# Separate PSUM tiles for inverse results and totals, earlier loads of batch 1, and a respread last stage in a Fourier and routing kernel

## The chip, the cores and the metric

One core of one Trainium2 chip runs the whole program. The metric is device time in microseconds (us) of one execution, the median of several. TensorE is called PE here, VectorE DVE, ScalarE ACT, GpSimd POOL and SyncE SP, as the profile names them.

## The reference, cut to what matters

Eight batches of x (3136 by 256) go through a real FFT along the sequence, a complex linear layer with a soft threshold, and the inverse FFT. Then a gate scores every row, the 128 rows of highest score in each batch go through a two-layer network, and their result is added with a sigmoid gate.

```
X = rfft(x, axis=1)
Yr = soft(Xr @ w_r - Xi @ w_i + b_r, 0.01)
Yi = soft(Xr @ w_i + Xi @ w_r + b_i, 0.01)
y = irfft(Yr + 1j*Yi, n=3136, axis=1)
scores = y @ w_gate
top = the 128 rows of highest score of each batch
out = y;  out[top] += sigmoid(scores[top]) * (relu(y[top] @ w1) @ w2)
```

## The kernel before, in words

The length 3136 is split as 98 by 32. Each batch passes through these stages, as matmuls against small tables:

- `ld_x` loads a pair of column groups into one of two `xts` tiles (of batch 0, the second half into the two `cvs` tiles), three DMAs each; `fold` adds and subtracts the two halves (POOL, in batch 0 partly DVE); `s1` multiplies (8 matmuls into PSUM tile `s`), ACT copies the result to SBUF, and three DMAs store a pair of results to the scratch `As`. There are U = 8 units `i` per batch.
- `ld_a` reads `As` back in another order, and `s2` makes the spectrum of group `g` (G = 13 groups per batch, the last one narrow): 32 matmuls into `px`, ACT casts the high part `Xh` (L450), DVE subtracts for the low part `Xl` (L451).
- `spectral` multiplies with the weights in three products of six matmuls: `k1` first (into `pc`), which ACT copies to `ks` (L465) and POOL adds to the bias in `kb` (L467), then two into `py`, to which DVE adds `kb` (L471).
- `shrink` is the soft threshold: ACT makes `r` (L476), DVE makes `Y` (L478).
- `s2i` is the first inverse stage of a group: 16 matmuls (L496, the narrow group L500) into `pc`, an ACT copy of both halves to `ct` (L502), and for each half a DVE multiply-and-sum with the gate vector (L505) that leaves the scores of the group in `Csc`. `ct` is stored to the scratch `Cs`.
- `ld_c` reads `Cs` back, and `s1i` is the last inverse stage (8 matmuls into `s`, L544, and an ACT copy to `ot`, L546); pairs are stored to the output (L553, L554).
- `route` (one generator per batch) makes the scores (`score`), finds the threshold four bits at a time (`select`: nine rounds, each a matmul of totals, L244, read by DVE, L247 or L254, and two longer DVE counts, L237 and L241) and the row numbers (`place`, L267 to L314). Its matmuls write `sel_ps` and `route_ps`, which are columns of `pc`.
- `fetch` gathers the 128 rows (L322), and `ffn` runs the network on them (`prepare`, `hidden`, `combine`) and scatters them.

[...] `pc` is one tile of two banks with four users: the left half of its first bank and the left half of its second are the two halves of the result of `s2i`, the right half of the first is `sel_ps` and `route_ps`, and the right half of the second is `k1`. The waits between engines are made by the tile framework, from which instructions read and write a tile.

The order on every engine is the order in which the program is written (`manual_schedule`). After a prologue for batch 0, one loop runs over steps `t`. A step flushes the pending stores and issues the loads (all on SP's queue), and then runs: `s2` of group t+1; `pair` (one `s1` or `s1i`); `tick(threads)`, which moves every active route generator on by one yield; `spectral` of group t, with a second tick after `k1`; the folds; `tick(ffns)`; `s2i` of group t-1; `shrink` of group t; and `pair` again. So a route generator moves by two yields a step, and its totals matmul stands on PE's queue between `s2` and `k1`. Batch 1 runs its `s1` by the table `first` during the first steps, later batches LEAD = 17 steps ahead by `steady`, and `s1i` follows LAG = 18 steps behind, eight units in 13 steps.

Of the kernel before, what the change touches and what calls it, by code (L numbers as in the profile page):

```python
# [10 lines left out]
F32 = mybir.dt.float32  # L11
# [8 lines left out]
B, S, D = 8, 3136, 256  # L20
# [80 lines left out]
def fourier_moe(ctx: ExitStack, tc: tile.TileContext, x, w_r, w_i, b_r, b_i, wg, w1, w2,  # L101
# [11 lines left out]
    xv = x.rearrange("b (h m c) d -> b m h c d", h=2, c=N2)  # L113
    ov = [o.rearrange("(a r c i) d -> c a r (i d)", r=16, c=2, i=2) for o in outs]
    As, Cs, xt, sd, at, ct, av, cv, ot, X, Y, Csc = [{} for _ in range(12)]
    pc = ps.tile([128, 2, 512], F32, name="pc", bufs=1)

    def c_tile(shape, dt, name):
        return const.tile(shape, dt, name=name)
# [26 lines left out]
    def ld(out, src):  # L146
        nc.sync.dma_start(out=out, in_=src)

    sel_ps, route_ps = pc[:, 0, D:D + 64], pc[:, 0, D + 64:]

    w3 = []

# [220 lines left out]
    def ld_x(b, i):  # L373
        if i % 2:
            return
        k = i // 2
        t = xt[b, k] = (cvs if b == 0 and k > 1 else xts)[k % 2].rearrange("p (h c) d -> p h c d", h=2)
        for r in range(2):
            ld(t[64 * r:64 * r + 48], xv[b, :48, :, 8 * k + 4 * r:8 * k + 4 * r + 4, :])
        ld(t[48:113:64], xv[b, 48, :, 8 * k:8 * k + 8, :].rearrange("h (r c) d -> r h c d", r=2))  # L380

# [71 lines left out]
    def spectral(b, g, between):  # L453
        r = 128 if width(g) == 2 else NF
        xh, xl = X.pop((b, g))

        def product(out, c, w):
            for h in range(2):
                mm3(out, xh[:, h, c, :], xl[:, h, c, :], w[0][:, h, :], w[1][:, h, :], start=(h == 0), stop=(h == 1))

        k1 = pc[:, 1, D:]
        py = ps.tile([128, 2, D], F32, name="py", bufs=1)
        product(k1, 2, wts[0])
        ks = pool.tile([128, 1, D], F32, name="ks", bufs=2)
        nc.scalar.copy(out=ks[:r, 0, :], in_=k1[:r])  # L465
        kb = pool.tile([128, 2, D], F32, name="kb", bufs=KB)
        nc.gpsimd.tensor_tensor(out=kb[:r], in0=ks[:r].broadcast_to([r, 2, D]), in1=bias[:r], op=ALU.add)  # L467
        between()
        product(py[:, 0, :], 1, wts[2])
        product(py[:, 1, :], 0, wts[1])  # L470
        nc.vector.tensor_tensor(out=py[:r], in0=py[:r], in1=kb[:r], op=ALU.add)  # L471
        return py, r
# [8 lines left out]
    def s2i(b, g):  # L481
        w = width(g)
        if g == 0:
            Cs[b] = dram.tile([NH, 64, D], F32, name="Cs")
            Csc[b] = pool.tile([128, NJ], F32, name="Csc")
            nc.vector.memset(Csc[b][:, NJ - 1:], 0.0)
        if g % 2 == 0:
            ct[b] = pool.tile([128, 4, D], F32, name="ct", bufs=3)
        y = Y.pop((b, g))
        r = 128 if w == 2 else 64  # L490
        p = pc[:, :, :D]
        if w == 2:
            for c in range(2):
                for q in range(2):
                    for a in range(2):
                        nc.tensor.matmul(p[64 * a:64 * a + 64, q, :], gi_sb[64 * q:64 * q + 64, g, c, 64 * a:64 * a + 64], y[64 * q:64 * q + 64, c, :],  # L496
                                         start=(c == 0), stop=(c == 1))
        else:
            for c in range(2):
                nc.tensor.matmul(p[:64, 0, :], gti_sb[:, c, :], y[:64, c, :], start=(c == 0), stop=(c == 1))  # L500
        o = 2 * (g % 2)
        nc.scalar.copy(out=ct[b][:r, o:o + w, :], in_=p[:r, :w])  # L502
        for k in reversed(range(w)):
            junk = pool.tile([128, D], F32, name="junk", bufs=1)
            nc.vector.tensor_tensor_reduce(out=junk[:r], in0=p[:r, k, :], in1=wgb[:r], scale=1.0, scalar=0.0,  # L505
                                           op0=ALU.mult, op1=ALU.add, accum_out=Csc[b][:r, 2 * g + k:2 * g + k + 1])
        t = ct[b]
        if w == 1:
            stores.append(lambda: nc.sync.dma_start(out=Cs[b][48], in_=t[:r, o, :]))
        elif g % 2 == 1:  # L510
            stores.append(lambda: nc.sync.dma_start(out=Cs[b][:48].rearrange("(j q) n d -> (q n) j d", q=2)[:, 2 * g - 2:2 * g + 2], in_=t))
# [15 lines left out]
    def ld_c(b, i):  # L527
        if i % 2:
            return
        k = i // 2  # L530
        t = cv[b, k] = (xts if b == B - 1 and k > 1 else cvs)[k % 2]
        for r in range(2):
            ld(t[64 * r:64 * r + 48], Cs[b][:48, 16 * k + 8 * r:16 * k + 8 * r + 8, :])
        ld(t[48:113:64], Cs[b][48, 16 * k:16 * k + 16].rearrange("(r n) d -> r n d", r=2))

    def s1i(b, i):
        e = i % 2
        if e == 0:
            ot[b] = pool.tile([128, 2, 2, 2 * D], F32, name="ot", bufs=2)
        f = cv[b, i // 2]  # L540
        p = ps.tile([128, 2, 2 * D], F32, name="s", bufs=1)
        for r in range(2):
            for c in range(2):
                nc.tensor.matmul(p[64 * c:64 * c + 64, r, :], w[64 * r:64 * r + NH, 2, :], f[64 * r:64 * r + NH, 4 * e + 2 * c:4 * e + 2 * c + 2, :], start=True, stop=True)  # L544
        t = ot[b]
        nc.scalar.copy(out=t[:, :, e, :], in_=p)  # L546
        if e == 0:
            return

        def store():  # L550
            n = slice(2 * i - 2, 2 * i + 2)
            for c in range(2):
                nc.sync.dma_start(out=ov[b][c, :48, n, :], in_=t[64 * c:64 * c + 48].rearrange("p r s x -> p (r s) x"))  # L553
            nc.sync.dma_start(out=ov[b][:, 48, n, :], in_=t[48:113:64].rearrange("p r s x -> p (r s) x"))  # L554
        stores.append(store)

    def warm():
        pf = pool.tile([128, 512], F32, name="Y", bufs=YB)
        nc.vector.memset(pf, 0.5)
        pr = pool.tile([128, 768], F32R, name="Xh", bufs=XB)  # L560
        nc.scalar.copy(out=pr[:, :512], in_=pf)
        p = ps.tile([128, 2, 512], F32, name="px", bufs=1)
        for i in range(30):
            nc.tensor.matmul(p[:, i % 2], pr[:, :128], pr[:, :512], start=True, stop=True)

    HB, YB, XB, KB, RB = 2, 2, 2, 1, 1
# [6 lines left out]
    def route(b):  # L573
        while done["s2i"] < b:
            yield
            yield
        yield
        yield
        yield from score(b)
        yield from select(b, 4, thrs)  # L580
        yield from place(b, thrs[b], slots)
# [50 lines left out]
    for i in range(U):  # L632
        fold(0, i, nc.gpsimd if i % 3 == 2 else nc.vector)
        s1(0, i)
        flush()
    weights()
    warm()
    ld_a(0, 0)
    consts_g(1)
    first = {i * 10 // U: i for i in range(U)}  # L640
    ld_x(1, 0)
    ld_x(1, 2)
    fold(1, 0, nc.gpsimd)
    fold(1, 1, nc.gpsimd)
    for t in range(-1, B * G + LAG + 1):
        flush()
        for b, i in steady(t + LEAD + 4):
            ld_x(b, i)
        if t + 2 in first and first[t + 2] > 2:
            ld_x(1, first[t + 2])  # L650
        if 1 < t + 3 < B * G:
            ld_a(*divmod(t + 3, G))
        for b, i in due(t - LAG + 2, U):
            ld_c(b, i)
        if t % 2 == 0 and (t + 4) // 2 in range(2, 7):
            consts_g((t + 4) // 2)
        if t == -1:
            consts_gi(0)
        if t % 2 and (t + 1) // 2 in range(0, 6):
            consts_gi((t + 1) // 2 + 1)  # L660
        if t == 8:
            consts_b()
        if t % 2 == 0:
            consts_moe((t - 14) // 2)
            split_moe((t - 18) // 2)
        if 0 <= t + 1 < B * G:
            s2(*divmod(t + 1, G))
        pairs = [(s1, b, i) for b, i in steady(t + LEAD)]
        if t in first:
            pairs.append((s1, 1, first[t]))  # L670
        pairs += [(s1i, b, i) for b, i in due(t - LAG, U)]

        def pair():
            if pairs:
                f, b, i = pairs.pop(0)
                f(b, i)
                if f is s1i and i == U - 1:
                    done["s1i"] = b

        pair()  # L680
        tick(threads)
        if 0 <= t < B * G:
            py, r = spectral(*divmod(t, G), lambda: tick(threads))
        else:
            tick(threads)
        for b, i in steady(t + LEAD + 2):
            fold(b, i, nc.gpsimd)
        if t + 2 in first and t >= 0:
            fold(1, first[t + 2], nc.gpsimd)
        tick(ffns)  # L690
        if 0 <= t - 1 < B * G:
            s2i(*divmod(t - 1, G))
            if (t - 1) % G == G - 1:
                done["s2i"] = (t - 1) // G
        if 0 <= t < B * G:
            shrink(*divmod(t, G), py, r)
        pair()
# [31 lines left out]
```

## Time and profile before

| what | us |
|---|---|
| median of three runs (902.44 to 913.03) | 906.48 |
| the profiled execution's own time | 905.22 |
| its span, first to last instruction | 903.4 |
| PE busy in the span | 700.4 |
| DVE, ACT, POOL busy | 501.2, 365.2, 309.3 |

The profiled execution is 1.8 us longer than its span and 1.3 us under the median. Busy times are unions over an engine's instructions. In a timeline row, a bracket gives the idle time of that engine before the row and what ended it. In a row of groups, the number behind the second bar is the idle time of the engine just before that group, with what ended it. In a row by stretch stand its two ends, its length, the busy time and count of PE, of its weight loads, of DVE, ACT and POOL, then the granted clock of PE (1 is 2.4 GHz), the DMA share and the rate in GB/s. DMA share is the mean busy share of the 16 DMA engines, and it can exceed 1 where packets overlap on an engine.

### The profile page before, as it was taken

To read this page: it belongs to the slowest core of one execution; us is meant where nothing else is said; L and a number is where in the kernel's file an instruction comes from. 1 tells how busy PE (TensorE), PEld (TensorE's weight loads), DVE (VectorE), ACT (ScalarE), POOL (GpSimd) and SP (SyncE) were. 2 spreads that over 40 slices of the span, in tenths; PEclk is the share of its full clock that TensorE was granted. 3 is DMA by queue.
4 is the path that set the end of the run, shared out by engine and by line. 5 is a ranking of instruction groups with operands and counts; after the bars stand their busy time and mean duration, and the time that the engine had idled before them with its cause. 6 is when DMAs were issued, how large, how long until landed. Compare 5 with 4: busy or idle time off the path is not lost.

```text
span 903.4 us, 20480 instructions
## 1 busy us (share of the span) xinstructions
PE 700.4 (78%) x8302; PEld 516.7 (57%) x8302; DVE 501.2 (55%) x1369; ACT 365.2 (40%) x579; POOL 309.3 (34%) x272
## 2 busy tenths in 40 slices
PE   4788798887877887788878887878878787678574
PEld 1456576555655665556655665656656666565243
DVE  4334455666367645675467645675466644774631
ACT  2244454445345444444344444444444333333120
POOL 3063654355433423443334424443232211221000
PEclk9889799999899999999999999999999998999567
DMA  8889989989887978977797977978786635755840
GB/s 166 231 184 225 248 196 218 239 197 249 198 199 192 211 160 200 226 173 177 176 212 198 211 169 186 223 170 198 168 185 158 158 87 139 156 138 118 188 112 14
DMA packets 87868, 163.83 MB, mean 181 GB/s; under 512 B 7809, under 2 KB 61052, under 8 KB 81502
## 3 DMA queue, kind: packets, MB, share of 16 engines
q1 hardware_dynamic: 86734, 160.26, 75.5%
q0 software_dynamic: 896, 2.17, 0.8%
q8 instruction: 65, 1.06, 0.5%
q14 instruction: 29, 0.24, 0.1%
q10 hardware_dynamic: 144, 0.10, 0.0%
HBM read 84.45 MB, written 78.12 MB: 180 GB/s over the span
## 4 chain that ended last, share of the span: by engine, by line
PE 43%; DVE 19%; ACT 9%; DMA 5%; issue 5%; POOL 1%; SPq 1%; POOLq 0%; ACTq 0%
PE pc L496 8%; DVE Xl L451 6%; DVE junk L505 6%; PE pc L218 5%; PE py L218 5%; PE py L219 5%; PE py L220 5%; ACT ct L502 4%; DVE Y L478 4%; PE m L347 3%; PE s L544 3%; PE pc L220 2%; PE pc L219 2%; ACT ot L546 2%; DMA cv<-Cs 2%
## 5 line engine op out<-in xcount | busy, mean ns | idle before, releaser
L467 POOL TENSOR_TENSOR kb<-ks,bias 128x512 f32<-128x512 f32 (+1 forms) x104 | 133.1, 1280 | 447.7 <-ACT ks L465 447.7
L471 DVE TENSOR_TENSOR py<-py,kb 128x512 f32<-128x512 f32 (+1 forms) x104 | 72.7, 699 | 196.0 <-POOL kb L467 127.4
L387 POOL TENSOR_TENSOR sd<-xt 113x512 f32<-113x512 f32 x114 | 143.3, 1278 | 48.7 <-DMA xt<-in_x 48.7
L502 ACT COPY ct<-pc 128x512 f32<-128x512 f32 (+1 forms) x104 | 59.0, 567 | 228.0 <-PE pc L496 215.9
L218 PE MATMUL pc<-wsh,Xh 128*128 128x256 f32 x208 | 74.1, 356 | 90.2 <-DVE ok L254 59.2
L505 DVE CUSTOM_DVE_ANT_0 junk<-pc,wgb 128x256 f32<-128x256 f32 (+1 forms) x200 | 84.8, 424 | 87.7 <-ACT ct L502 83.3
L218 PEld LDWEIGHTS pc<-wsh,Xh 128*128 128x128 f32 x208 | 42.9, 206 | 124.4 <-DVE ok L254 61.7
L496 PE MATMUL pc<-Y,gi_sb 64*64 64x256 f32 x1536 | 106.1, 392 | 0.0
L451 DVE TENSOR_TENSOR Xl<-px,Xh 128x768 fp32r<-128x768 f32 x96 | 91.2, 950 | 26.8 <-ACT Xh L450 26.3
L465 ACT COPY ks<-pc 128x256 f32<-128x256 f32 (+1 forms) x104 | 38.7, 372 | 148.0 <-PE pc L220 146.8
L444 PEld LDWEIGHTS px<-g_sb,av 64*64 64x64 f32 x3072 | 78.9, 134 | 29.9 <-issue 13.5
L444 PE MATMUL px<-g_sb,av 64*64 64x96 f32 x3072 | 85.4, 245 | 9.8 <-DMA av<-As 7.2
L398 PE MATMUL s<-sd,w 49*64 49x512 f32 x480 | 74.6, 647 | 20.7 <-DVE sd L387 10.4
L450 ACT CAST Xh<-px 128x768 fp32r<-128x768 f32 x96 | 76.9, 801 | 12.3 <-PE px L444 12.3
L546 ACT COPY ot<-s 128x1024 f32<-128x1024 f32 x64 | 65.1, 1017 | 38.0 <-PE s L544 31.9
L544 PE MATMUL s<-cv,w 49*64 49x512 f32 x480 | 71.5, 631 | 10.7 <-ACT ot L546 8.2
L476 ACT ACTIVATE r<-py,m2l 128x512 f32<-128x512 f32 (+1 forms) x104 | 71.8, 691 | 13.0 <-DVE py L471 13.0
L478 DVE SCALAR_TENSOR_TENSOR Y<-py,r 128x512 f32<-128x512 f32 (+1 forms) x104 | 71.3, 686 | 1.9 <-ACT r L476 1.8
L400 ACT COPY at<-s 128x1024 f32<-128x1024 f32 x58 | 59.7, 1030 | 22.9 <-PE s L398 22.9
L496 PEld LDWEIGHTS pc<-Y,gi_sb 64*64 64x64 f32 x1536 | 49.9, 134 | 25.6 <-issue 2.4
L218 PE MATMUL py<-wnh,Xh 128*128 128x256 f32 x208 | 63.9, 307 | 0.0
L220 PE MATMUL py<-wnl,Xh 128*128 128x256 f32 x208 | 63.9, 307 | 0.0
(128 smaller groups left out, 1352.6 us busy)
## 6 DMA issues: line engine op xcount, KB each, us to landing
av<-As SPq DMA_DIRECT2D x96, 256.0 KB
Cs<-ct SPq DMA_DIRECT2D x48, 512.0 KB
out<-ot SPq DMA_DIRECT2D x64, 384.0 KB
xt<-in_x SPq DMA_DIRECT2D x60, 384.0 KB
As<-at SPq DMA_DIRECT2D x60, 384.0 KB
cv<-Cs SPq DMA_DIRECT2D x60, 384.0 KB
cv<-in_x SPq DMA_DIRECT2D x4, 384.0 KB
As<-ot SPq DMA_DIRECT2D x4, 384.0 KB
```

Source lines behind the costliest of these rows:

```text
L218: nc.tensor.matmul(out, wh, mh, start=start, stop=False)
L220: return nc.tensor.matmul(out, wh, ml, start=False, stop=stop).ins
L387: eng.tensor_tensor(out=f[:113, k], in0=t[:113, 0], in1=t[:113, 1], op=op)
L444: nc.tensor.matmul(o[:, :, N2 * j:N2 * j + N2], a[64 * p:64 * p + 64, 2 * (g % 2) + j, 128 * h + 64 * q:128 * h + 64 * q + 64], g_sb[64 * ...
L451: nc.vector.tensor_tensor(out=vl, in0=v, in1=vh.bitcast(F32), op=ALU.subtract)
L467: nc.gpsimd.tensor_tensor(out=kb[:r], in0=ks[:r].broadcast_to([r, 2, D]), in1=bias[:r], op=ALU.add)
L478: nc.vector.scalar_tensor_tensor(out=y[:r], in0=py[:r], scalar=0.0, in1=r1[:r], op0=ALU.min, op1=ALU.add)
L496: nc.tensor.matmul(p[64 * a:64 * a + 64, q, :], gi_sb[64 * q:64 * q + 64, g, c, 64 * a:64 * a + 64], y[64 * q:64 * q + 64, c, :], start=(c ...
L502: nc.scalar.copy(out=ct[b][:r, o:o + w, :], in_=p[:r, :w])
L505: nc.vector.tensor_tensor_reduce(out=junk[:r], in0=p[:r, k, :], in1=wgb[:r], scale=1.0, scalar=0.0, op0=ALU.mult, op1=ALU.add, accum_out=C ...
L544: nc.tensor.matmul(p[64 * c:64 * c + 64, r, :], w[64 * r:64 * r + NH, 2, :], f[64 * r:64 * r + NH, 4 * e + 2 * c:4 * e + 2 * c + 2, :], st ...
L546: nc.scalar.copy(out=t[:, :, e, :], in_=p)
```

## The change

Three parts. In PSUM, the tile `pc` becomes two tiles of one bank, `pca` (first half of the `s2i` result, `sel_ps`, `route_ps`) and `pcb` (second half, `k1`); the ACT copy of the `s2i` result becomes two, the second half first, each followed by its DVE sum. At the beginning, two `ld_x` of batch 1 are issued among the stores of batch 0, the table `first` starts one step later and runs one unit per step, the other loads of batch 1 are issued earlier against it, and the warm-up has 14 matmuls for 30. At the end, `route` yields twice less, `s1i` runs one unit per step once the last group is through, the loads of the last batch stand in two groups (the first pair into the `xts` tiles), its `s1i` results take two `at` and two `ot` tiles, and its odd units write `px` for `s`.

```diff
-    pc = ps.tile([128, 2, 512], F32, name="pc", bufs=1)
+    pca, pcb = [ps.tile([128, 2 * D], F32, name=n, bufs=1) for n in ("pca", "pcb")]
...
-    sel_ps, route_ps = pc[:, 0, D:D + 64], pc[:, 0, D + 64:]
+    sel_ps, route_ps = pca[:, D:D + 64], pca[:, D + 64:]
...
-        for r in range(2):
+        for r in (1, 0):
             ld(t[64 * r:64 * r + 48], xv[b, :48, :, 8 * k + 4 * r:8 * k + 4 * r + 4, :])
...
-        k1 = pc[:, 1, D:]
+        k1 = pcb[:, D:]
...
-        p = pc[:, :, :D]
+        p = [t[:, :D] for t in (pca, pcb)]
...
-        nc.scalar.copy(out=ct[b][:r, o:o + w, :], in_=p[:r, :w])
         for k in reversed(range(w)):
+            nc.scalar.copy(out=ct[b][:r, o + k, :], in_=p[k][:r])
             junk = pool.tile([128, D], F32, name="junk", bufs=1)
-            nc.vector.tensor_tensor_reduce(out=junk[:r], in0=p[:r, k, :], in1=wgb[:r], scale=1.0, scalar=0.0,
+            nc.vector.tensor_tensor_reduce(out=junk[:r], in0=p[k][:r], in1=wgb[:r], scale=1.0, scalar=0.0,
...
-        t = cv[b, k] = (xts if b == B - 1 and k > 1 else cvs)[k % 2]
+        t = cv[b, k] = (xts if b == B - 1 and k < 2 else cvs)[k % 2]
...
-            ot[b] = pool.tile([128, 2, 2, 2 * D], F32, name="ot", bufs=2)
+            ot[b] = pool.tile([128, 2, 2, 2 * D], F32, name="at" if b == B - 1 and i < 4 else "ot", bufs=2)
...
-        p = ps.tile([128, 2, 2 * D], F32, name="s", bufs=1)
+        p = ps.tile([128, 2, 2 * D], F32, name="px" if b == B - 1 and e else "s", bufs=1)
...
-        for i in range(30):
+        for i in range(14):
             nc.tensor.matmul(p[:, i % 2], pr[:, :128], pr[:, :512], start=True, stop=True)
...
         while done["s2i"] < b:
             yield
             yield
-        yield
-        yield
         yield from score(b)
...
         s1(0, i)
+        if i == 4:
+            ld_x(1, 0)
+            ld_x(1, 2)
         flush()
...
-    first = {i * 10 // U: i for i in range(U)}
-    ld_x(1, 0)
-    ld_x(1, 2)
+    first = {i + 1: i for i in range(U)}
...
-    for t in range(-1, B * G + LAG + 1):
+    rest = [(b, i) for b in range(B) for i in range(U)]
+    for t in range(-1, B * G + 20):
...
-        if t + 2 in first and first[t + 2] > 2:
-            ld_x(1, first[t + 2])
+        if t + 4 in first and first[t + 4] > 3:
+            ld_x(1, first[t + 4])
...
         for b, i in due(t - LAG + 2, U):
-            ld_c(b, i)
+            if b < B - 1:
+                ld_c(b, i)
+        if t in (B * G + 1, B * G + 3):
+            for i in range(4):
+                ld_c(B - 1, i + 2 * (t - B * G - 1))
...
-        pairs += [(s1i, b, i) for b, i in due(t - LAG, U)]
+        for _ in due(t - LAG, U) if t < B * G else rest[:1]:
+            pairs.append((s1i, *rest.pop(0)))
...
-        if t + 2 in first and t >= 0:
+        if t + 2 in first and first[t + 2] > 1:
             fold(1, first[t + 2], nc.gpsimd)
```

## Rows read from the trace of the kernel before

**Rows 1.** Busy time by stretch of the span (windows); columns told above.

```profile
0.00:52.30 52.30, 30.78 (x167) 13.70 (x167) 20.72 (x27) 11.49 (x12) 13.65 (x14) 0.89 0.90 195
52.30:131.70 79.40, 68.13 (x909) 50.87 (x907) 37.19 (x87) 37.91 (x62) 43.96 (x42) 0.90 0.91 215
131.70:219.00 87.30, 70.57 (x945) 52.45 (x945) 55.77 (x145) 43.05 (x72) 40.61 (x36) 0.96 0.95 224
219.00:728.50 509.50, 408.27 (x5115) 310.14 (x5115) 299.60 (x839) 223.07 (x355) 186.78 (x159) 0.95 0.79 188
...
485.95:492.54 6.59, 5.13 (x75) 3.78 (x75) 4.93 (x14) 3.15 (x5) 3.76 (x3) 1.00 0.55 139
...
728.50:817.90 89.40, 67.06 (x856) 53.50 (x856) 54.70 (x155) 33.38 (x57) 18.06 (x16) 0.96 0.55 131
817.90:903.40 85.50, 55.56 (x317) 36.03 (x317) 33.20 (x120) 16.31 (x22) 6.23 (x6) 0.69 0.47 109
```

**Rows 2.** Groups of PE's instructions by line, 219 to 728.5 us, with idle before.

```profile
L218 PE MATMUL pc<-wsh,Xh 128*128 128x256 f32 x131 | 47.9, 365 | 63.8 <-DVE ok L254 44.4 <-DVE w L247 9.6 <-DVE row L291 6.6
L544 PE MATMUL s<-cv,w 49*64 49x512 f32 x328 | 46.8, 599 | 5.8 <-ACT ot L546 5.8
...
L398 PE MATMUL s<-sd,w 49*64 49x512 f32 x288 | 37.7, 592 | 5.5 <-ACT ot L546 5.5
...
L244 PE MATMUL pc<-n,tm 98*98 98x15 bf16 (+2 forms) x45 | 9.2, 205 | 11.6 <-DVE idx L314 4.9 <-DVE Csc L505 2.6
...
L522 PE MATMUL pc<-sct,wq 25*98 25x32 f32 x40 | 4.4, 249 | 6.8 <-DVE cnt L283 6.8
```

**Rows 3.** Timeline of one selecting step: start us, us, engine, line, operation.

```profile
487.00 0.37 ACT L465 COPY ks<-pc 128x256 f32<-128x256 f32 x1 [1.40 <-PE pc L220]
...
488.26 1.09 PE L496 MATMUL pc<-Y,gi_sb 64*64 64x256 f32 x16
...
489.42 0.59 ACT L502 COPY ct<-pc 128x512 f32<-128x512 f32 x1 [2.04 <-PE pc L496]
...
489.84 1.04 PE L398 MATMUL s<-sd,w 49*64 49x512 f32 x8
...
490.04 0.42 DVE L505 CUSTOM_DVE_ANT_0 junk<-pc,wgb 128x256 f32<-128x256 f32 x1 [0.57 <-ACT ct L502]
...
490.51 0.42 DVE L505 CUSTOM_DVE_ANT_0 junk<-pc,wgb 128x256 f32<-128x256 f32 x1
...
491.00 0.21 PE L244 MATMUL pc<-n,tm 98*98 98x15 bf16 x1
...
491.46 0.95 DVE L451 TENSOR_TENSOR Xl<-px,Xh 128x768 fp32r<-128x768 f32 x1
492.33 0.16 DVE L254 TENSOR_SCALAR ok<-pc 98x15 f32<-98x15 f32 x1
...
492.55 0.39 PE L218 MATMUL pc<-wsh,Xh 128*128 128x256 f32 x1 [1.34 <-DVE ok L254]
```

**Rows 4.** Timeline of the beginning, PE, SP and POOL.

```profile
33.59 9.00 PE L564 MATMUL px<-Xh 128*128 128x512 f32 x30 [5.09 <-ACT Xh L561]
...
36.17 2.62 SPq L147 DMA_DIRECT2D av<-As  x2
...
39.49 3.04 SPq L147 DMA_DIRECT2D xt<-in_x  x6
...
47.81 4.92 POOL L387 TENSOR_TENSOR sd<-xt 113x512 f32<-113x512 f32 x4 [23.90 <-DMA xt<-in_x]
...
94.33 0.58 PE L444 MATMUL px<-g_sb,av 64*64 64x96 f32 x4 [4.33 <-DMA av<-As]
```

**Rows 5.** Timeline of the end: the last row numbers and the gather.

```profile
878.86 0.15 DVE L314 TENSOR_TENSOR idx<-col,pc 128x1 uint32<-128x1 f32 x1
882.77 0.96 POOL L322 DMA_INDIRECT xe<-out,idx  x1 [6.88 <-DMA out<-ot]
```

More of the change, by code (lines that the diff above doesn't have):

```diff
@@ L495, in s2i @@
                     for a in range(2):
-                        nc.tensor.matmul(p[64 * a:64 * a + 64, q, :], gi_sb[64 * q:64 * q + 64, g, c, 64 * a:64 * a + 64], y[64 * q:64 * q + 64, c, :],
+                        nc.tensor.matmul(p[q][64 * a:64 * a + 64], gi_sb[64 * q:64 * q + 64, g, c, 64 * a:64 * a + 64], y[64 * q:64 * q + 64, c, :],
                                          start=(c == 0), stop=(c == 1))
@@ L499, in s2i @@
             for c in range(2):
-                nc.tensor.matmul(p[:64, 0, :], gti_sb[:, c, :], y[:64, c, :], start=(c == 0), stop=(c == 1))
+                nc.tensor.matmul(p[0][:64], gti_sb[:, c, :], y[:64, c, :], start=(c == 0), stop=(c == 1))
         o = 2 * (g % 2)
-        nc.scalar.copy(out=ct[b][:r, o:o + w, :], in_=p[:r, :w])
         for k in reversed(range(w)):
+            nc.scalar.copy(out=ct[b][:r, o + k, :], in_=p[k][:r])
             junk = pool.tile([128, D], F32, name="junk", bufs=1)
-            nc.vector.tensor_tensor_reduce(out=junk[:r], in0=p[:r, k, :], in1=wgb[:r], scale=1.0, scalar=0.0,
+            nc.vector.tensor_tensor_reduce(out=junk[:r], in0=p[k][:r], in1=wgb[:r], scale=1.0, scalar=0.0,
                                            op0=ALU.mult, op1=ALU.add, accum_out=Csc[b][:r, 2 * g + k:2 * g + k + 1])
```

## The prediction

> **What bounds the kernel now.** I read three views in this order: the busy time by stretch, the groups of PE in the steady part, and the timeline of one step. The stretches show PE as the engine nearest to full: 408.3 of 509.5 us in the five batches from 219 to 728.5, against 299.6 on DVE [rows 1]. So what is worth asking is where the other 101.2 us of PE go. The groups answer it: 63.8 us stand in front of the first `k1` matmul of a step (130 steps, the 131st belongs to the next batch), ended by DVE reading `ok`, `w` or `row`; 11.3 wait for an ACT copy of `s`; 11.6 and 6.8 stand before routing matmuls [rows 2]. The timeline shows why. `ok` reads the totals in `pc`, and on DVE it is queued behind `Xl`, which belongs to the next group's spectrum. `k1` needs neither, but it writes `pc` too. The totals matmul was done at 491.21, `ok` ended at 492.49, and `k1` began at 492.55 [rows 3]. In the first 130 us, before any routing, another thing binds: DMA at a share of 0.9 [rows 1].
>
> [...] The row: `k1` writes the second bank of `pc`, the totals lie in the first, and still it starts 0.06 us after `ok` ends [rows 3]. [...]
>
> **Two PSUM tiles: one selecting step.** It lasts 6.59 us, from `k1` at 485.95 to `k1` at 492.55 [rows 1, 3]. From `k1` to the end of the inverse matmuls (488.26 + 1.09 = 489.35) are 3.40 us, which stay. From there to the next `k1` are 3.20. In the new order ACT copies a half, 0.37 us by the `ks` row of the same shape, from 489.42 to 489.79; the first sum of DVE starts at 489.81 where it started at 490.04, and the second 0.47 later, ending at 490.70. The totals matmul starts 0.07 behind that, as before, and not ahead of the end of the `s1` matmuls (490.88, less an overlap of some 0.1): at 490.8. `k1` (in `pcb`) now waits only for the first sum and stands right behind it: 490.95, 1.60 after the inverse [rows 3]. Step: 3.40 + 1.60 = 5.0. DVE takes the place of the wait: its work in this step is 4.93 us and ten joints of 0.03 [rows 1], so 5.0 becomes 5.15 or more, a saving of 1.44.
>
> Who else is touched: the next inverse matmuls write `pca` and wait for `ok`; it ends 3.14 us after the last inverse (492.49), they start 1.60 + 2.31 = 3.91 after it, so 0.8 us of cover. If DVE falls behind by more, that time is paid there. The second ACT copy costs 0.37 + 0.37 - 0.59 = 0.15 us at most 0.41 where copies don't overlap; ACT is busy 223 of 509.5 [rows 1], and `r` behind it moves by 0.04 to 0.2, hidden since `Y` stands behind both sums on DVE's queue.
>
> **The five steady batches.** Of PE's idle 101.2 us the 63.8 before `k1` go, and 2.6 before the totals that waited for `Csc` [rows 2]. What stays: waits for `ot` copies 11.3, for `idx` 4.9, `cnt` 6.8 and most of the 7.7 in smaller groups, where two routes are in one step and the second route's matmul still waits for the first's DVE read in `pca` [rows 2]. Bounds of what goes: 0 and 101. I take 66 (the rows' own sum). The granted clock is 0.95 over this stretch [rows 1]: 25 us of clock are lost, in spells at the lower level, 1.2 GHz, which in the trace follow the steps with most idle time of PE. Between 0 and 25 I take 11, as more than half of that idle time goes. Denser steps ask more of the DMA: share 0.79 over 509.5 us is 402 us of all 16 engines [rows 1], which in 437 us would be 0.92. The part from 131.7 to 219 ran at 0.95 [rows 1], so it fits, with late loads now and then: 0 to 22 (one of 4.33 per batch, [rows 4]), I take 5. 509.5 - 66.4 - 11 + 5 = 437.
>
> [...]
>
> **The other stretches.** 131.7 to 219: idle of PE 87.3 - 70.6 = 16.7 [rows 1]; but the DMA share of 0.95 is 83 us of work, and at 1.04, the most that I allow for a whole batch, 80. From 87.3 to 80. 728.5 to 817.9: idle 22.3, and little DMA (0.55); by `k1`'s part of the idle time in the steady stretch (63.8 of 101.2) it loses 14, and 2 less as this batch thins out at its end (bounds 0 and 22): 77.5.
>
> 52.3 to 131.7: no routing yet. PE idle is 11.3, of which 4.3 is one wait for `av`, at 94; SP had issued it late, behind a load of batch 2 that waited for a fold, which waited for the load of unit 4 [rows 1, 4]. That load goes out two steps before its old distance, so the wait goes. Half-clock time goes with it (clock 0.90: up to 8 us). DMA share 0.91 is 72 us of work [rows 1], at 1.04 69: I take 71, so -8.4 (bounds -10 and 0).
>
> 0 to 52.3: the two `ld_x` of batch 1 are six issues of SP, 3.04 us; from the first, at 39.5, to the fold that waited for them, at 47.8, were 8.3 us, and in the first step `s1` of batch 1 waited for that fold [rows 4]. That wait goes: `k1` of step 0 no longer has this `s1` ahead. But the bytes now stand on SP's queue before half of batch 0's stores and the first `av`: 8.3 us of transfers, less some 2 of the 5 that a share of 0.90 leaves free [rows 1], so `av` is issued at 42.5 for 36.2. It landed between 38.8 and the end of the warm-up at 42.6 [rows 4]; I take 5 us from issue, and an estimated 3.8 from there to `k1` (two spectra, and a cast and a subtraction between): 51.3 for 52.3, and half a microsecond of it back for the clock, since PE is now idle ahead of `s2`. The 16 warm-up matmuls less are under this wait. So -0.5 (bounds -4 and +4).
>
> 817.9 to 903.4: the gather waited from 879.0 to 882.8 for the last output store [rows 5]; with `s1i` one per step it is through seven steps earlier, so 3.8 goes. `route` is one step earlier, some 2.4 us, but PE waits for the first load of the last batch's `Cs` in either order. I take -6 (bounds -3 and -11). The gather, the network and the scatter behind it, 21 us, stay.
>
> **Sum.** 51.8 + 71 + 80 + 437 + 77.5 + 79.5 = 796.8 of span, with 1.8 around it 798.6: I say 798. The profiled execution (905.22) is 1.3 under the median of 906.48, which I leave.
>
> **Rivals.**
> 1. DMA becomes the bound. For: shares of 0.9 to 0.95 where the kernel is young, and one wait for `av` of 4.3 us [rows 1, 4]. Against: in the steady part none of PE's large waits is for a DMA [rows 2]. One such late load per batch in six batches is 26 more: 824.
> 2. PE stays at full clock and the DMA keeps up: the five batches lose 71 and 25, not 66 and 11, and none for DMA (-24), the two batches around them 10 more: 764.
> 3. The wait is not the tile's: `k1` still starts behind `ok`. For: the different banks. Against: each of its releasers reads other columns of `pc` than it writes, and a route's `row` and `w` hold it as `ok` does [rows 2]. Then only the ends gain, 8.4 + 0.5 + 6: 890.
> 4. Slower: the wait stays as in 3, and ACT's two copies do not overlap. Place: copy, `r`, `Xh`, `Xl`, `ok`, `k1`. Each of 96 wide groups then pays 0.2, 19 us, and the early loads of batch 1 put `av` 4 us late (the upper bound above) without the gain of batch 0: 905 + 19 + 4 - 6 = 922. It decides only if `k1` still stands behind `ok`.
>
> **How the numbers follow.** The forecast (780 to 815) gets 0.48, rival 1 0.24, rival 2 0.20, rival 3 0.05, rival 4 0.03. A measurement here tells about 1% from no change, 9 us. Rivals 1 and 2 and the forecast are all faster; rival 3 too by 1.8%, but if the ends give nothing it is no change, so I put 0.03 of it there and 0.02 on faster. Faster 0.94, same 0.03, slower 0.03. The range reaches to 760 for rival 2 and to 846 for rival 1 with two late loads a batch, or with no clock won.
>
> **What would show it.** Right: the idle time before `k1` falls from 63.8 to under 10 us in the five batches; a plain selecting step takes 5.0 to 5.3; the idle time moves to routing matmuls that wait for DVE, with DVE busy over 65% there; a batch takes some 87 us; no long wait for `av` in the first ten steps; the gather starts right behind the last `idx`. Wrong: `k1` still behind `ok`; or PE groups waiting for `av`, `cv` or `sd` in every batch with a DMA share over 1; or a granted clock under 0.93 in the steady part.

## The result, and where it differs from the prediction

The changed kernel takes 843.37 us (838.65 to 847.18, four runs) against 908.81 for the kernel before in the same session: a ratio of 0.928, 95% interval 0.920 to 0.936. It is faster, as forecast, and inside the range, but 45 us above the predicted 798. The profiled execution took 845.35 us, with a span of 843.6.

The busy time by stretch, changed kernel, cut at the same places of the program as [rows 1]:

```profile
0.00:50.63 50.63, 24.68 (x142) 10.88 (x142) 19.74 (x26) 10.80 (x11) 14.14 (x14) 0.82 0.91 219
50.63:122.32 71.69, 66.62 (x918) 49.69 (x915) 38.20 (x88) 38.70 (x75) 43.64 (x41) 0.94 0.99 219
122.32:209.30 86.98, 74.15 (x948) 56.28 (x945) 66.39 (x148) 42.60 (x82) 40.56 (x35) 0.88 0.91 216
209.30:681.99 472.69, 400.20 (x5126) 308.75 (x5123) 354.17 (x842) 226.49 (x418) 192.82 (x160) 0.94 0.86 205
681.99:765.09 83.10, 66.95 (x861) 54.67 (x857) 62.65 (x159) 34.94 (x69) 18.23 (x16) 0.94 0.62 147
765.09:843.56 78.47, 52.47 (x309) 32.55 (x308) 32.41 (x116) 16.32 (x23) 6.23 (x6) 0.72 0.48 119
```

| stretch | before | forecast | measured | off by |
|---|---|---|---|---|
| to the first `k1` | 52.3 | 51.8 | 50.6 | -1.2 |
| batch 0 | 79.4 | 71 | 71.7 | +0.7 |
| batch 1 | 87.3 | 80 | 87.0 | +7.0 |
| the five steady batches | 509.5 | 437 | 472.7 | +35.7 |
| the last batch of steps | 89.4 | 77.5 | 83.1 | +5.6 |
| the end | 85.5 | 79.5 | 78.5 | -1.0 |

The beginning, batch 0 and the end came out as forecast. All that is missing is in the three stretches in which column selection runs beside spectral steps, and in these DVE's busy time (third of the five) has risen, in the five batches from 299.6 to 354.2 us, for the same instructions. DVE as a whole went from 501.2 to 573.5 us.

PE's groups in the five steady batches, to be laid beside [rows 2]:

```profile
L496 PE MATMUL pca<-Y,gi_sb 64*64 64x256 f32 x480 | 68.1, 404 | 4.0 <-DVE w L247 4.0
...
L444 PE MATMUL px<-g_sb,av 64*64 64x96 f32 x1920 | 52.7, 243 | 0.8 <-DMA av<-As 0.8
L544 PE MATMUL s<-cv,w 49*64 49x512 f32 x328 | 47.9, 611 | 8.7 <-ACT ot L546 5.6 <-DMA cv<-Cs 3.0
L218 PE MATMUL pcb<-wsh,Xh 128*128 128x256 f32 x130 | 45.1, 347 | 0.0
...
L244 PE MATMUL pca<-n,tm 98*98 98x15 bf16 (+2 forms) x45 | 8.0, 178 | 40.7 <-DVE Csc L505 32.1 <-DVE idx L314 8.4
```

The 63.8 us in front of `k1` are gone to 0.0: the wait did go by tile, and two tiles remove it. But the totals matmul right ahead of `k1` now waits 40.7 us, 32.1 of them for the sums `Csc` at the end of DVE's queue, where it waited 11.6. So DVE is late, and its groups in the same stretch say with what (`c`, `w`, `f` and `hot` are results of the selection and of the row numbers; `n` is there to compare). Changed kernel:

```profile
L237 DVE TENSOR_TENSOR c<-scores,f 98x480 bf16<-98x480 f32 (+2 forms) x45 | 44.2, 982 | 1.5
...
L241 DVE TENSOR_REDUCE n<-c 98x15 bf16<-98x480 bf16 (+2 forms) x45 | 25.8, 574 | 1.6
...
L257 DVE SCALAR_TENSOR_TENSOR w<-d,w 98x1 uint32<-98x1 uint32 x40 | 23.4, 585 | 1.4
L234 DVE TENSOR_TENSOR f<-digits,w 98x15 uint32<-98x15 uint32 (+1 forms) x40 | 18.6, 464 | 1.4
L300 DVE SCALAR_TENSOR_TENSOR hot<-iota,end,hot 98x128 f32<-98x128 f32 x10 | 12.5, 1245 | 0.4
```

The kernel before, the same groups, 219 to 728.5 us:

```profile
L237 DVE TENSOR_TENSOR c<-scores,f 98x480 bf16<-98x480 f32 (+2 forms) x45 | 25.9, 576 | 1.5
L241 DVE TENSOR_REDUCE n<-c 98x15 bf16<-98x480 bf16 (+2 forms) x45 | 25.8, 574 | 1.6
...
L234 DVE TENSOR_TENSOR f<-digits,w 98x15 uint32<-98x15 uint32 (+1 forms) x40 | 6.9, 173 | 1.4
...
L257 DVE SCALAR_TENSOR_TENSOR w<-d,w 98x1 uint32<-98x1 uint32 x40 | 6.4, 159 | 1.4
L300 DVE SCALAR_TENSOR_TENSOR hot<-iota,end,hot 98x128 f32<-98x128 f32 x10 | 3.5, 351 | 0.4
```

`c`, `w`, `f` and `hot` have grown by 56.0 us (98.7 less 42.7), as much as DVE gained in the stretch (54.6). What they share: each reads two tiles in SBUF. `n`, of the same width as `c` but with one input, stayed at 574 ns, and what reads one of its inputs from PSUM (`py`, `Xl`, the sums) kept its length within 1%. One step of the changed kernel, in its timeline (start us, us, engine, line, operation), shows when it happens:

```profile
453.52 0.17 PE L244 MATMUL pca<-n,tm 98*98 98x15 bf16 x1
453.55 0.36 PE L218 MATMUL pcb<-wsh,Xh 128*128 128x256 f32 x1
...
454.02 0.96 DVE L451 TENSOR_TENSOR Xl<-px,Xh 128x768 fp32r<-128x768 f32 x1
...
454.89 0.16 DVE L254 TENSOR_SCALAR ok<-pca 98x15 f32<-98x15 f32 x1
...
455.25 1.28 POOL L467 TENSOR_TENSOR kb<-ks,bias 128x512 f32<-128x512 f32 x1 [3.60 <-DMA out<-ot]
...
455.29 1.25 DVE L257 SCALAR_TENSOR_TENSOR w<-d,w 98x1 uint32<-98x1 uint32 x1
...
456.49 2.50 POOL L387 TENSOR_TENSOR sd<-xt 113x512 f32<-113x512 f32 x2
...
456.58 1.21 DVE L234 TENSOR_TENSOR f<-digits,w 98x15 uint32<-98x15 uint32 x1
...
457.83 1.67 DVE L237 TENSOR_TENSOR c<-scores,f 98x480 bf16<-98x480 f32 x1
...
461.75 0.17 PE L244 MATMUL pca<-n,tm 98*98 98x15 bf16 x1 [3.31 <-DVE Csc L505]
```

`w` is one column, 0.16 us of work. It starts while POOL adds `kb` and ends at 456.54, 0.01 after `kb`. `f` starts in the first half of POOL's fold and ends with it; `c` starts in the second half, which ends at 458.99, and then takes 0.5 us more. So these instructions do not run slower: they stand until POOL's instruction is through. Counted over the whole trace, 25 of the 64 `w` start while POOL is in `kb` or a fold; each of these ends 12 to 23 ns behind POOL's instruction, and none of the other 39 takes over 161 ns. In the kernel before, of all 200 `w`, `f` and `c` none starts there. The step is 8.2 us long, where 5.15 was forecast; a step with the same PE work takes 6.59 in the kernel before. The step just ahead of it, from 448.6, has `w`, `f` and `c` through in 0.16, 0.18 and 0.66 us and takes 4.96.

Why the two meet now: `ks`, and `kb` behind it, follow `k1`; `w`, `f` and `c` follow `ok`. Before, `k1` stood behind `ok`, so `w`, `f` and `c` were through before `kb` began, 1.5 us after `k1` at 485.95. The kernel before, in the step of [rows 3]:

```profile
486.14 0.16 DVE L257 SCALAR_TENSOR_TENSOR w<-d,w 98x1 uint32<-98x1 uint32 x1
...
486.33 0.17 DVE L234 TENSOR_TENSOR f<-digits,w 98x15 uint32<-98x15 uint32 x1
...
486.54 0.66 DVE L237 TENSOR_TENSOR c<-scores,f 98x480 bf16<-98x480 f32 x1
...
487.45 1.29 POOL L467 TENSOR_TENSOR kb<-ks,bias 128x512 f32<-128x512 f32 x1 [2.83 <-ACT ks L465]
```

Now `k1` begins 1.34 us ahead of `ok` (453.55 and 454.89), and takes `kb` with it. The removed wait had kept them apart.

Over the five batches `w` takes a mean of 585 ns for 159 (up to 1.26 us in the whole trace, for one column), while `n` is untouched at 574; e7 below shows the other order. The prediction had not reckoned with this.

### The profile page after: what moved, and what is told of

Read it like the earlier page. It is cut to its first block, busy times and chain, and to the rows that moved or that the text cites. A ratio compares the mean times of both kernels' runs of the same rounds, so it can differ in the third digit from the quotient of the medians.

```text
span 843.6 us, 20678 instructions
## 1 busy us (share of the span) xinstructions
PE 685.1 (81%) x8286; PEld 512.8 (61%) x8286; DVE 573.5 (68%) x1369; ACT 369.9 (44%) x675; POOL 315.6 (37%) x272
## 4 chain that ended last, share of the span: by engine, by line
PE 37%; DVE 34%; DMA 14%; issue 6%; ACT 6%; SPq 1%; POOL 1%; POOLq 0%; DVEq 0%; ACTq 0%
PE pca L496 6%; DVE Xl L451 6%; DVE junk L505 5%; DMA av<-As 5%; DVE c L237 5%; PE py L218 3%; DVE Y L478 3%; PE py L219 3%; PE py L220 3%; DVE py L471 3%; DMA As<-at 3%; DVE w L257 3%; PE pcb L218 3%; DMA xt<-in_x 3%; PE s L544 3%
## 5 line engine op out<-in xcount | busy, mean ns | idle before, releaser
L387 POOL TENSOR_TENSOR sd<-xt 113x512 f32<-113x512 f32 x114 | 146.4, 1305 | 20.4 <-DMA xt<-in_x 20.4
L503 ACT COPY ct<-pcb 128x256 f32<-128x256 f32 x96 | 35.7, 371 | 199.2 <-PE pcb L496 195.9
L496 PE MATMUL pca<-Y,gi_sb 64*64 64x256 f32 x768 | 108.9, 404 | 4.7 <-DVE w L247 4.7
L496 PE MATMUL pcb<-Y,gi_sb 64*64 64x256 f32 x768 | 108.8, 404 | 0.0
L218 PEld LDWEIGHTS pcb<-wsh,Xh 128*128 128x128 f32 x208 | 43.1, 207 | 71.9 <-issue 58.2
L398 PE MATMUL s<-sd,w 49*64 49x512 f32 x480 | 70.2, 624 | 17.5 <-DVE sd L387 9.5
L544 PE MATMUL s<-cv,w 49*64 49x512 f32 x464 | 69.8, 632 | 13.9 <-ACT ot L546 10.0
L218 PE MATMUL pcb<-wsh,Xh 128*128 128x256 f32 x208 | 73.0, 351 | 0.0
L237 DVE TENSOR_TENSOR c<-scores,f 98x480 bf16<-98x480 f32 (+2 forms) x72 | 65.7, 913 | 2.5
L496 PEld LDWEIGHTS pca<-Y,gi_sb 64*64 64x64 f32 x768 | 47.7, 139 | 32.5 <-DVE w L247 5.7
L546 ACT COPY ot<-s 128x1024 f32<-128x1024 f32 x58 | 59.3, 1022 | 14.8 <-PE s L544 14.8
```

What stands on the lines that cost most here:

```text
L218: nc.tensor.matmul(out, wh, mh, start=start, stop=False)
L237: nc.vector.tensor_tensor(out=c, in0=sv.broadcast_to([N1, m, N2]), in1=f.bitcast(F32).rearrange("p (m o) -> p m o", o=1).broadcast_to([N1, ...
L387: eng.tensor_tensor(out=f[:113, k], in0=t[:113, 0], in1=t[:113, 1], op=op)
L496: nc.tensor.matmul(p[q][64 * a:64 * a + 64], gi_sb[64 * q:64 * q + 64, g, c, 64 * a:64 * a + 64], y[64 * q:64 * q + 64, c, :], start=(c == ...
```

## The experiments

**The two halves of the change.** e1 is the kernel before with the two tiles alone; e2 is the changed kernel with the one tile of before.

```diff
-    pc = ps.tile([128, 2, 512], F32, name="pc", bufs=1)
+    pca, pcb = [ps.tile([128, 2 * D], F32, name=n, bufs=1) for n in ("pca", "pcb")]
...
-        nc.scalar.copy(out=ct[b][:r, o:o + w, :], in_=p[:r, :w])
         for k in reversed(range(w)):
+            nc.scalar.copy(out=ct[b][:r, o + k, :], in_=p[k][:r])
```

> The kernel before with the two PSUM tiles and the two ACT copies alone. Theory A (the removed wait let DVE's selecting instructions slide under POOL's kb and folds, where they run longer): the steady part behaves as in the changed kernel, 219 to 728.5 us falls from 509.5 to about 473, the beginning and the end stay, total 860 to 870, with the mean of L237 near 0.9 us. Rival B (the changed kernel is held by late DMAs that its earlier loads of batch 1 brought): without them the steady part should come nearer to the forecast, 437, total 840 or less. Rival C (most of the gain is from the ends): 890 or more.

> The changed kernel with the one tile of two banks and the one ACT copy put back: beginning and end alone. By the stretches of the two profiles they should give 1.6 (to the first k1), 7.7 (batch 0) and 7 (end): total 888 to 896. Theory A: the mean of L237 is back at 0.58 us, since k1 waits for ok again. Rival C: 860 or less.

e1 took 885.42 us, ratio 0.976 (0.971 to 0.981); e2 took 894.46, ratio 0.986 (0.981 to 0.991). e2 came out as expected. e1 gained less than expected. Its DVE is as busy as the changed kernel's (574.4 us), and its `k1` wait is as much gone (0.6 us in the whole span); but the five batches take 503.8 us. So the parts, by their ratios some 22 and 13 us, do not add up to the 65 of the whole, and the missing 30 are looked for below (e8, e11).

**POOL's work taken out.** e3 is the changed kernel without the folds of batches 2 to 7 and without `kb`; e4 does the same to the kernel before.

```diff
-        nc.gpsimd.tensor_tensor(out=kb[:r], in0=ks[:r].broadcast_to([r, 2, D]), in1=bias[:r], op=ALU.add)
...
-        for b, i in steady(t + LEAD + 2):
-            fold(b, i, nc.gpsimd)
```

> The changed kernel with POOL's steady work left out: the folds of batches 2 to 7 (their s1 reads the last fold of batch 1 instead) and the kb addition (DVE adds the bias alone; the share of k1 is left out). Theory A: L237 back to a mean of 0.58 us, L257 to 0.16, L234 to 0.17, five steady batches near the forecast (425 to 445 for 473), total 785 to 805. Rival B (DMA is the bound): no more than 10 us less than the changed kernel, with the DMA share over 1 in the steady part and PE waiting for av, cv.

> The kernel before with the same POOL work left out (folds of batches 2 to 7, kb). Control. Theory A: POOL cost nothing before, as the wait for ok kept DVE's selecting work ahead of kb: total within 1.5% of before (895 to 915), L237 at 0.58 us in both. If POOL's work itself were on the path in both kernels (rival D: py waits for kb), the time falls here as much as in the changed kernel, by 30 us or more.

e3: 788.16 us, ratio 0.870 (0.862 to 0.878). e4: 910.74, ratio 1.007 (1.004 to 1.010). Both are as expected: the same POOL work is worth 55 us in the changed kernel and nothing in the kernel before. DVE's busy time in e3 is 497.3 us, and `w` has its length back:

```profile
L257 DVE SCALAR_TENSOR_TENSOR w<-d,w 98x1 uint32<-98x1 uint32 x64 | 10.2, 160 | 2.2
```

**One POOL instruction at a time.** e5 leaves out `kb` alone, e6 the folds alone.

> The changed kernel with POOL's kb left out: each selecting step subtracts the plain bias in place of ks plus bias, so the choice of columns is another one, and the folds stay. If POOL's reads of SBUF lengthen the DVE instructions that read two SBUF tiles at the same moment (theory A), then w (the Xl subtraction), which runs beside kb, falls from a mean of 570 ns to 160 to 250, f and c stay long because the folds stay, and of the 55 us that both together were worth some 25 to 35 go: 808 to 822. If only the folds matter, 838 to 848; if it is the amount of POOL work and not its place, the two single experiments split the 55 us by busy time, kb's 130 pieces of 1.28 us against 64 folds of 2.5 us, and w stays as long as before.

> The changed kernel with the folds of batches 2 to 7 left out: those batches read the last fold of batch 1, so their outputs are other numbers, and kb stays. Theory A: f and c (and the difference of the gate, L300) fall back to their lengths of before, w stays at 500 ns or more, and 20 to 30 us go: 813 to 825. If only kb matters, 838 to 848.

e5: 802.97 us (two runs), so `kb` was worth 40 us, more than expected. e6: 825.67 (two runs), so the folds were worth 18, just less than expected. DVE's groups of e5, over the whole span:

```profile
L237 DVE TENSOR_TENSOR c<-scores,f 98x480 bf16<-98x480 f32 (+2 forms) x72 | 44.5, 619 | 2.5
...
L234 DVE TENSOR_TENSOR f<-digits,w 98x15 uint32<-98x15 uint32 x64 | 18.1, 283 | 2.2
L257 DVE SCALAR_TENSOR_TENSOR w<-d,w 98x1 uint32<-98x1 uint32 x64 | 14.3, 223 | 2.2
```

And of e6:

```profile
L237 DVE TENSOR_TENSOR c<-scores,f 98x480 bf16<-98x480 f32 (+2 forms) x72 | 45.3, 629 | 2.5
...
L257 DVE SCALAR_TENSOR_TENSOR w<-d,w 98x1 uint32<-98x1 uint32 x64 | 40.9, 639 | 2.2
L234 DVE TENSOR_TENSOR f<-digits,w 98x15 uint32<-98x15 uint32 x64 | 17.7, 276 | 2.2
```

In the changed kernel these means are 913, 405 and 570 ns. With the folds out, `w` stays long: it meets `kb`. With `kb` out, 13 of the 64 `w` meet a fold and the others are short, and `f` and `c` shrink too although the folds stay: 7 and 3 of them start while POOL works, for 15 and 24 in the changed kernel. There all 6 `f` and 6 of the 16 `c` that start in a fold stand behind a `w` held by `kb`, which had pushed them into it; why the other `c` meet it was not followed up. Neither run brings `f` and `c` back to the 173 and 576 ns of before. POOL's busy time falls by 134 us in e5 and by 121 in e6, nearly alike, but the kernel gains 40 and 18, so it is the place and not the amount. (In the recorded expectation of e5, `w` is L257 and not the subtraction of `Xl`, and the trace has 104 `kb` and 48 folds left out, not 130 and 64.)

**The order on DVE's queue.** If `ok` to `n` stood ahead of `Xl`, they would be through before `kb`. e7 issues the subtraction of `Xl` behind the second tick of the routes:

```diff
-        nc.vector.tensor_tensor(out=vl, in0=v, in1=vh.bitcast(F32), op=ALU.subtract)
+        return lambda: nc.vector.tensor_tensor(out=vl, in0=v, in1=vh.bitcast(F32), op=ALU.subtract)
...
-            s2(*divmod(t + 1, G))
+        low = s2(*divmod(t + 1, G)) if 0 <= t + 1 < B * G else lambda: None
...
-            py, r = spectral(*divmod(t, G), lambda: tick(threads))
+            py, r = spectral(*divmod(t, G), lambda: (tick(threads), low()))
```

> The changed kernel with the Xl subtraction put on DVE's queue behind the second tick in place of ahead of it, so that the reading of the totals and the chain behind it (ok to n) do not stand behind Xl and are through before kb starts on POOL. Theory A: a plain selecting step takes 5.2 to 5.6 us, w still meets kb but at the end of the queue, and the time is 800 to 825. If the order on DVE does not matter and only its sum does, the lengthening moves from c to w and the time is 838 to 850. If Xl comes too late for the next group's spectrum, PE waits for it in each step and the time is over 850.

779.07 us (776.35 to 784.78), ratio 0.860 (0.852 to 0.867): 64 us faster than the changed kernel, more than was expected, with all of POOL's work in place. Its stretches, from batch 0 on:

```profile
53.08:125.98 72.90, 67.05 (x918) 50.15 (x914) 38.27 (x88) 38.86 (x75) 43.65 (x41) 0.94 0.94 217
125.98:198.92 72.94, 67.26 (x948) 49.44 (x944) 54.06 (x148) 42.31 (x82) 40.14 (x35) 1.00 1.00 253
198.92:624.37 425.45, 385.96 (x5127) 289.65 (x5123) 301.63 (x842) 226.12 (x418) 190.63 (x160) 0.98 0.93 227
624.37:697.64 73.27, 64.86 (x860) 52.09 (x857) 54.80 (x159) 34.68 (x69) 19.26 (x16) 0.98 0.68 166
```

DVE is back at 301.6 us in the five batches, the clock at 0.98, and the same three stretches take 73, 425 and 73 us (forecast: 80, 437 and 77.5). One step of its timeline:

```profile
425.04 0.16 DVE L257 SCALAR_TENSOR_TENSOR w<-d,w 98x1 uint32<-98x1 uint32 x1
...
425.24 0.17 DVE L234 TENSOR_TENSOR f<-digits,w 98x15 uint32<-98x15 uint32 x1
...
425.44 0.66 DVE L237 TENSOR_TENSOR c<-scores,f 98x480 bf16<-98x480 f32 x1
...
425.94 1.31 POOL L466 TENSOR_TENSOR kb<-ks,bias 128x512 f32<-128x512 f32 x1 [1.32 <-ACT ks L464]
...
426.70 0.95 DVE L450 TENSOR_TENSOR Xl<-px,Xh 128x768 fp32r<-128x768 f32 x1
```

`c` is issued before `kb`, and what now runs beside `kb` and the fold, `n` and `Xl`, has at most one input in SBUF and keeps its length. The step that took 8.2 us, and 6.59 before, now takes 5.1 to 5.3 in each of the five batches. POOL is held in its turn: where an addition or fold starts with at least 0.15 us of a `c` still to run, which are 44 cases, it ends 1.13 to 1.15 us behind that `c`, so the longest takes 1.73 us for 1.28. Here that costs little, since `c` is short. Leaving POOL's work out had won 55 us (e3), so some 9 of the 64 come from elsewhere in the new order; they were not followed up.

**Which part of the wait was the tile, which the queue?** e7 put `ok` ahead of `Xl`, and the prediction had named both as reasons for the `k1` wait. So e9 gives e7 the one tile of before, and e10 is the kernel before with nothing but e7's edit.

> The order of e7 (Xl behind the second tick) with the one PSUM tile of before, all else as changed. ok now stands first on DVE's queue behind the totals, so k1 would wait for ok alone: in e7 the totals matmul began at 439.29, ok ended at 439.71 and k1 began at 439.36; with one tile k1 would begin some 0.4 us later, or 0.6 to 0.8 where ok stands behind Y. Over the 64 digit steps, and with the waits for row and w of the routes (some 20 us in one tile) still there, 30 to 45 us: 808 to 825 if the two tiles keep a worth of their own. If the order on the queue was the whole of it, the time stays at 775 to 790. If the split is worth as much as without the new order (51 us), 825 to 835.

> The kernel before with only the Xl subtraction behind the second tick. If the k1 wait of before came as much from ok standing behind Xl as from the shared tile, the wait before k1 falls from 90 to some 45 us and the time to 855 to 875. If the new order helps only by keeping two-input DVE work clear of POOL (theory A alone), nothing changes here, where the selection ended before kb: 895 to 912. If the later Xl holds up the next spectrum, over 915.

e9: 824.71 us, ratio 0.910 (0.903 to 0.917), at the upper end of what was expected if the tiles keep a worth of their own, and near what was expected if they lose none of it: 46 us beside e7, where 51 had been put for the tiles in the old order. e10: 836.64, ratio 0.922 (0.914 to 0.930), better than any theory had it. Moving one instruction behind the six of the selection on DVE's queue is worth as much as the whole change (0.928, 0.920 to 0.936). The `k1` group over the whole span, in the kernel before, e10 and e9:

```profile
L218 PE MATMUL pc<-wsh,Xh 128*128 128x256 f32 x208 | 74.1, 356 | 90.2 <-DVE ok L254 59.2 <-DVE w L247 12.9 <-DVE row L291 7.9
...
L218 PE MATMUL pc<-wsh,Xh 128*128 128x256 f32 x208 | 71.4, 343 | 43.4 <-DVE ok L254 24.0 <-DVE w L247 6.7 <-DVE Csc L504 4.4
...
L218 PE MATMUL pc<-wsh,Xh 128*128 128x256 f32 x208 | 71.1, 342 | 42.2 <-DVE ok L254 23.5 <-DVE w L247 6.9 <-DVE Csc L504 3.2
```

The new order alone takes 46.8 of the 90.2 us away: that part was `ok` standing behind `Xl`. The rest is the shared tile: 42.2 us in e9 are 0.3 in e7, which has two tiles and differs in nothing else. That e10's time fell by more than its `k1` wait (by 66.6 us) is in part PE's busy time, 14.2 us shorter in the whole span; the remainder was not followed up.

**Where the 30 us between the parts went.** The changed kernel's ends contain two yields fewer at the head of `route`, so every selection falls one step earlier. e8 puts them back in the changed kernel, e11 in e7.

```diff
             yield
+        yield
+        yield
         yield from score(b)
```

> The changed kernel with the two yields at the head of route put back: every batch's routing is one step later, as before, and all else is as changed. The split alone won 23 us and the ends alone 12 us, both together 65. If the missing 30 us come from where the routing falls against the steps that have two fourier pairs, folds or a feed-forward piece (theory A at other meetings: the splits-only run has one step of 12 to 13 us and one of 10.3 us in each batch), then this kernel loses most of them: the five steady batches about 500 us, the whole 865 to 876. If they come from the earlier loads of batch 1, it stays at 840 to 850.

> e7 with the two yields at the head of route put back, as e8 did to the changed kernel. If the 32 us that e8 lost came from more meetings of two-input DVE work with POOL (theory A), then here, where w, f and c run before kb, there is little to meet: 775 to 795, DVE busy within 10 us of e7's 500. If the place of the routing costs by other ways (two-pair steps, feed-forward pieces, half-clock time), it loses most of it again: 800 to 815.

e8: 875.83 us, ratio 0.967 (0.960 to 0.975): the two yields cost 32 us, and the five batches take 499.1, like e1's 503.8. So the missing 30 us are the place of the selection, not the early loads. But the reason given for it was half right: DVE is no busier in e8 (576.5) than in the changed kernel (573.5). There are not more meetings (74 of the `w`, `f`, `c` and `hot` start while POOL is in `kb` or a fold, 71 in the changed kernel); they fall into other steps. PE's groups of e8, five batches:

```profile
L544 PE MATMUL s<-cv,w 49*64 49x512 f32 x328 | 49.9, 631 | 20.0 <-ACT ot L546 17.3 <-DMA cv<-Cs 2.7
...
L398 PE MATMUL s<-sd,w 49*64 49x512 f32 x288 | 40.3, 631 | 12.5 <-ACT ot L546 12.5
```

The waits for copies of `s` rose from 10.0 us (5.6 and 4.4) to 29.8, as ACT's copies stand behind `r`, which waits for DVE's late `py` (2.33 us in the step at 458, whose `L544` then waits 3.17 for the copy); and the granted clock fell from 0.94 to 0.90, with 12.6 us more of busy time on PE. e11: 793.50 us (786.09 to 795.05), ratio 0.878 (0.872 to 0.883). In its profiled execution the five batches take 427.6 us against e7's 425.5, with DVE at 497.7 in all: without held DVE instructions the place of the selection costs them 2 us and not 26. By the medians 14 us remain between e11 and e7; what these are was not settled.

## Why the prediction was right, and where its sum failed

**Bound and mechanism: right.** PE's idle time was in front of `k1`, the wait went by tile, and it fell from 63.8 us to 0.0. (The five batches have 65 steps and not 130: a step has two matmuls of this group.) Rival 3 falls with that, and rival 4, which rested on it. e9 shows it from the other side: with one tile `k1` waits for `ok` again though the banks differ (42.2 us before `k1` over the span, 23.5 of them for `ok`; 0.3 in e7). Between e9 and e7 the two tiles saved 46 us: the order that this kernel keeps goes by tile. That the time lies inside the range of 760 to 846 is in part luck: the upper end was put there for late loads or a clock not won, and what filled it is a cost that no term of the sum has.

**The step that failed** is in "Two PSUM tiles": "DVE takes the place of the wait: its work in this step is 4.93 us and ten joints of 0.03, so 5.0 becomes 5.15 or more". That DVE would be next was right. (The sum itself gives 5.23, not 5.15.) Its 4.93 us were read from a step in which the wait itself kept the selection clear of POOL, and were carried into an order in which `kb` starts before `w`. In the step shown the same work takes 7.9 us of 8.2. Where DVE is not held the forecast of the step holds: 4.96 us in the step ahead of it, and 5.1 for the same step in e7. The prediction moved `k1` ahead by 1.4 us, and did not move `ks` and `kb` with it to see what they would then run beside.

**The five batches**, 437 forecast and 472.7 measured: PE's idle time was to be 39.8 us (101.2 less 66.4, and 5 for DMA) and is 72.5, which is 32.7 of the 35.7 missing; PE's busy time was to fall by 11 with the clock and fell by 8.1, though the granted clock did not rise (0.95, then 0.94). The lower level that the forecast counts is in the trace of the kernel before: in this stretch the clock is granted at 0.50 in 16 spells of 3.4 us and at 1.00 between them, 27 us lost, and in the 3.4 us ahead of a spell PE is busy for a share of 0.33 to 0.60, where the stretch has 0.80. The trace gives the clock as a share alone. At 0.50 the 256-column products of `spectral` start 213 ns apart, 1.2 columns a ns, and at 1.00 118 ns apart, 2.2 columns a ns (medians). So the 1.2 GHz of the forecast is an estimate that counts a column as a cycle, and 2.4 GHz for a full clock is its double. Of the terms, "2.6 before the totals that waited for `Csc`" was to go and became 32.1. The 5 us for DMA were near: PE waits 0.8 for `av` and 3.0 for `cv`. "0.8 us of cover" ahead of the next inverse held, for the most part: 4.0 us of waits in five batches.

**Batch 1 and the last batch of steps** missed by 7.0 and 5.6 for the same cause: in e7 they take 72.9 and 73.3, under the forecast.

**Batch 0, the beginning and the end** came out within 1.2 us each, though batch 0 not by all its steps: PE still waits 4.5 us for `av` in it, the wait of 4.33 that was to go [rows 4]. The gather at the end waits for the last row number, as forecast, where it waited for a store:

```profile
822.72 0.96 POOL L322 DMA_INDIRECT xe<-out,idx  x1 [2.60 <-DVE idx L314]
```

**Rivals.** Rival 1, the DMA as bound at 824, lies nearest to the measured time and is not what happened: PE waits 0.8 us for `av` and 3.0 for `cv` in the five batches, and e7 moves 227 GB/s there where the changed kernel moves 205. The highest rate of a stretch shown here is e7's 253 GB/s in batch 1, at a share of 1.00, short of the 1.04 that the forecast allowed for a whole batch (the kernel before has 1.04 from 18 to 21 us). Rival 2, full clock, 764, is what e7 comes near to (0.98 in the five batches, 779), once DVE is no longer held. What none of the rivals had was a cost on DVE that the removed wait had been hiding.

## What to carry to other kernels

Before a wait is removed, list what it keeps apart, not only who waits: all that follows the released instruction moves forward with it, here a copy on ACT and an addition on POOL, and may land on work whose duration was read from a trace where the two never met. And when an instruction waits for a result that is queued behind foreign work, try the order of that queue first: one moved instruction was worth as much here as the two tiles and all else of the change, and both together 127 us (e7, 905.92 in its session).

## What the runs showed of the hardware

In the changed kernel, `w`, `f`, `c` and `hot`, each with two inputs in SBUF, start 71 times while POOL runs an elementwise add on SBUF tiles, and 70 times do not end before POOL's instruction has (one `f`, begun 2 ns behind `kb`, kept its 0.17 us): 0.16 us of work took up to 1.26 us, ending 12 to 23 ns behind it in all 25 cases of `w`. It goes both ways: POOL's instruction keeps its length beside a `w` that starts after it (1.28 us), and when it starts during `c` it took up to 1.73 us, ending 1.13 to 1.15 us behind `c` (e7, 44 cases). `n`, with one input in SBUF, and `py` and `Xl`, with one there and one in PSUM, kept their mean lengths within 1% in every run. Since the held time counts as busy, it shows in the profile as DVE being fuller (501.2 to 573.5 us) and not as a wait; only the mean duration of a group, against another run, gives it away.
